# A cross network in two-level Winograd form: evicted blocks change buffers, and the second tile's transposes and loads change places

## The chip, the core and the metric

The kernel runs on one core of one Trainium2 chip. The metric is the device time of one execution in microseconds. The core has five engines that matter here: TensorE (PE) multiplies, ScalarE (ACT) and VectorE (DVE) work on tiles in SBUF and on the banks of PSUM in which PE leaves its results, GpSimd (POOL) and SyncE (SP) here mostly issue DMAs. Each engine runs its own program in order, and waits where a semaphore has not yet been raised.

## The reference: six cross layers

The input x0 has 16384 rows of 1024 features (bf16), there are six weight matrices of 1024 x 1024 and six biases. The output is x after the last layer.

```python
def reference(x0, ws, bs):
    x = x0
    L = ws.shape[0]
    for l in range(L):
        proj = jnp.einsum('bd,de->be', x, ws[l]) + bs[l]
        x = x0 * proj + x
    return x
```

## The kernel before

**Tiles and units.** Rows are cut into 16 tiles (`pr`) of 1024. Two tiles make a group, and the loop goes group by group, within a group layer by layer, and within a layer over the two tiles (`lane` 0 and 1). One tile in one layer is a unit: 96 units, numbered 0 to 95. Unit 12 g + 2 l + s is tile s of group g in layer l. So unit 37 is group 3, layer 0, second tile, and unit 38 is group 3, layer 1, first tile. The loop that writes all operations starts at line 268.

**Winograd.** In a unit x (1024 x 1024) and W (1024 x 1024) are each cut into four blocks of 512, and x W is done with seven block products instead of eight, P1 to P7. Each needs a weight block or a sum of such blocks, which the code names by the product ("1", "2", "4" raw; "5", "6", "7", "3" made by DVE). On the other side stand sums of x blocks, T1 to T4, made by DVE (lines 418 to 421). Three of the seven products (5, 2, 3), or four (also 4), are themselves done in seven quarter products, 5p1 to 5p7 and so on; their weight sums are "5i", "2i", "3i", "4i". Units of group 0's first tile and unit 95 are plain, that is without this second level; both tiles of layer 0 and the second tile of layers 1 to 4 have four inner products from group 1 on; the rest have three. A full product column is four matmuls of 512 columns at line 304 (`P1.0` is its first column group), an inner one four of 256 at line 492.

**Eviction.** PE writes eight PSUM banks, pA0 to pA3 and pX0 to pX3. ACT empties them: E1 into P1s, E6 into U, E7 into V, E4 into W (line 323, with the bias); the inner products by copies at line 313, of which some go from bank to bank (5f1, 5f2), some to `ip` (5e_p5), and some into a block (5e_c11, 5e_u0 and so on into 5c; the same for 2 into Q, 3 into 3c, 4 into W). The blocks are the seven tiles named `ev`: P1s, P5s (5c), Q, U, V, W, C3 (3c). Each role has its own fixed buffer (lines 171 and 172).

**After the products.** DVE adds the blocks up at line 199: 5cc, 2cc, 3cc, 4cc finish the inner products, then Q1 adds P1s to Q, Ua and Va add 5c to U and to V, Ub adds 3c to U, Wa adds V to W. Then Qm, Um, Vm, Wm multiply by x0. The old x is added last. In layers 1 to 4 that is an accumulating DMA of POOL for Q, U and V (`Qx`, `Ux`, `Vx`, lines 547 to 550), from the block into the state `xst`, and a DVE addition for W (`Wx`); in layer 5 DVE does all four; in layer 0 nothing, since the bias already has 1 added. So the buffer of U is read until Ux's DMA has landed, that of W until Wx is done.

**Weights.** Weight blocks pass through a ring of 12 slots (`wring`), in the order 1, 5, 5i, 2, 2i, 6, 3, 3i, 7, 4, 4i of each layer and group, and are used by both tiles. `pump` (line 234) issues a load on SP as soon as the oldest slot's last use has been emitted, so the load of a block waits, in SP's program, for a product of the second tile in the layer before: with 11 blocks to a layer and 12 slots, "5i" takes the slot of "5", "3i" that of "3". In group 0 only the raw blocks are loaded, DVE makes the sums and POOL saves them to DRAM (`Lc`).

**x0 and outputs.** x0 is kept in three tiles `x0T` and is loaded by transposing DMAs on SP, `ld` at line 328; those of the second tile are written in that tile's layer 0 unit (lines 341 to 343). A finished tile is transposed back by four DMAs `tro` (line 647) into a free x0T tile and stored by four `sto` (line 655). The first tile's output goes out in the second tile's layer 5 unit, that of the second tile (odd) in the next group's layer 0 unit of its second tile. After the odd tile's last `tro` POOL issues a tiny DMA, `fence` (line 338, tile `seen`), that waits for it; accumulating DMAs of POOL stand behind it.

**The order.** All operations are collected with the names of what they read and write (`op`, line 260). `schedule` (line 48) then simulates the five engines with the operations' `occ` (time on the engine) and `lat` (time to the result) and `at` (not before): PE follows the order written out at lines 17 to 36, every other engine takes the ready operation that is due first. The result is the order in which instructions are emitted, for all engines together (line 694). It sets each engine's program; on the chip the waits are by semaphores on the real buffers. `ARRIVE` holds the planner's assumed times of the first loads; an accumulating DMA is planned with a `lat` of 7.0 us.

Of the kernel before, what the change touches and what calls it, by code (L numbers as in the profile page):

```python
# [33 lines left out]
P1.0 P1.1 P1.2 P1.3 P2.0 P2.1 P2.2 P2.3 P5.0 P5.1 P5.2 P5.3 P6.0 P6.1 P6.2 P6.3 P3.0 P3.1 P3.2 P3.3 P7.0 P7.1 P7.2 P7.3  # L34
P4.0 P4.1 P4.2 P4.3 tV.0 tV.1 tV.2 tV.3 xW.0 tW.0 xW.1 tW.1 xW.2 tW.2 xW.3 tW.3
""".split()
ARRIVE = {"rows0": 4.9, "w0.1": 6.4, "rows1": 8.9, "rows2": 11.3, "w0.2": 11.9, "h0": 14.3, "h1": 15.5, "q": 17.5}


class Op:  # L40
# [85 lines left out]
def kernel(  # L126
# [12 lines left out]
    KH = KD // 2  # L139
    H = D // 2  # L140
# [28 lines left out]
    ip = {X: work.tile([P, KQ, KQ * P], BF16, name=f"ip{X}") for X in "523"}  # L169
    ip["4"] = ip["2"]  # L170
    P1s, P5s, Q, U, V, W, C3 = (work.tile([P, KH, KH, P], BF16, name=f"ev{i}") for i in range(7))
    CB = {"5": P5s, "2": Q, "3": C3, "4": W}
    TURNED, rows = ((0, 0), (1, 0), (0, 1)), (P1s, U, V)
    zeros = tin["4"][:, 0]
    ident = const.tile([P, P], BF16, name="ident")
# [45 lines left out]
    slot = {(gl, w): f"slot{i % RING}" for i, (gl, w, _) in enumerate(ring_seq)}  # L221
# [35 lines left out]
    ops, named = [], {}  # L257
    FAR = 1e9

    def op(name, eng, occ, lat, fn, rd=(), wr=(), weights=(), key=None, after=(), due=FAR, at=0.0):  # L260
        rd = tuple(rd) + tuple(slot[k] for k in weights if k in slot)
        for k in weights:
            uses_left[k] = uses_left.get(k, 0) + 1
        named[name] = len(ops)
        ops.append(Op(name, eng, occ, lat, fn, rd, tuple(wr), tuple(weights), key, tuple(named[a] for a in after), due, at))

    QD = ((0, 0), (0, 1), (1, 0), (1, 1))
    for u, (pr, l) in enumerate(units):
        one, first, last = plain(u), u == 0, u == NU - 1
        gl, grp, lane = gl_of(u), pr // 2, pr % 2  # L270
        x0T, xst = x0Ts[pr % 3], xsts[pr % 3]
        xs = x0T if l == 0 else xst
        X0 = {q: f"x0.{pr % 3}.{q[0]}{q[1]}" for q in QD}
        XO = {q: f"xs.{pr % 3}.{q[0]}{q[1]}" for q in QD}
# [14 lines left out]
        def dve(name, fn, n, rd, wr, weights=(), u=u, gl=gl, at=0.0, due=FAR):  # L289
            occ = n / 1920 + 0.068  # L290
            op(f"{name}@{u}", "DVE", occ, occ + 0.12, fn, rd, wr, [(gl, w) for w in weights], at=at, due=due)
# [33 lines left out]
        def load(pt, q, at=0.0, after=(), u=u):  # L325
            def fn():
                r0 = pt * PR + q[1] * NB
                nc.sync.dma_start_transpose(out=blk(x0Ts[pt % 3], *q), in_=x0[r0:r0 + NB, q[0] * H:(q[0] + 1) * H])
            op(f"ld{q[0]}{q[1]}.{pt}@{u}", "SP", 2.7, 6.0, fn, [], [f"x0.{pt % 3}.{q[0]}{q[1]}"], at=at, after=after)
# [10 lines left out]

        if l == 0 and lane == 1:
            for q in QD:
                load(pr, q, 17.0 if u == 1 else 0.0)

        if grp == 0 and lane == 0:
            raw = lambda w, gl=gl: wt[(gl, w)]

            def save(w, t, rd, weights=(), l=l, u=u, gl=gl):
                def fn():
                    nc.gpsimd.dma_start(Lc[l, CIDX[w]].rearrange("p (k e) -> p k e", k=KH), t())  # L350
                op(f"s{w}@{u}", "POOL", 1.0, 7.0, fn, rd + (["gate"] if u == 0 else []), (), [(gl, x) for x in weights])

            if first:
                ga = const.tile([P, 1], BF16, name="gate")

            def combo(w, a, b, o_, deps, gl=gl, raw=raw, first=first):
                def part(sl):
                    tt(raw(w)[:, :, sl], raw(a)[:, :, sl], raw(b)[:, :, sl], o_)

                def fn():  # L360
                    ring_make(gl, w)
                    part(slice(0, HQ) if w == "5" and first else slice(0, H))
                rd = [f"w{gl}.{d}" for d in deps]
                if w == "5" and first:
                    dve("c5", fn, KH * HQ, ["ringmake"], ["w0.5a", "ringmake", slot[gl, w]], [a, b], at=ARRIVE["h0"])
                    dve("c5b", lambda part=part: part(slice(HQ, H)), KH * HQ, ["w0.5a"], ["w0.5"], [a, b], at=ARRIVE["h1"])
                else:
                    dve("c" + w, fn, KH * H, rd + ["ringmake"], [f"w{gl}.{w}", "ringmake", slot[gl, w]], [a, b])
            combo("5", "w12", "4", ADD, ())
            combo("6", "5", "1", SUB, ("5",))  # L370
            combo("7", "1", "w12", SUB, ())
            combo("3", "2", "6", SUB, ("6",))
            for Xi in ISLOT:
                if Xi == "4i" and l not in K4:
                    continue
                X = Xi[0]
                a = lambda r, c, X=X, gl=gl: wt[(gl, X)][:, r * KQ:(r + 1) * KQ, c * HQ:(c + 1) * HQ]
                sv = isum(Xi).rearrange("p q (k e) -> p q k e", k=KQ)
                src = [] if X == "2" else [f"w{gl}.{5 if X == '4' else X}"]
                nm = lambda i, Xi=Xi: f"is.{Xi}.{i}"  # L380

                def icombo(i, fn, rd, Xi=Xi, X=X, src=src, nm=nm):
                    dve(Xi + i, fn, KQ * HQ, [nm(r) for r in rd] + src, [nm(i), ISN[Xi]], [X], at=ARRIVE["w0.2"] if first else 0.0)
                icombo("5", lambda a=a, sv=sv: tt(sv[:, 0], a(0, 1), a(1, 1), ADD), ())
                icombo("6", lambda a=a, sv=sv: tt(sv[:, 1], sv[:, 0], a(0, 0), SUB), "5")
                icombo("3", lambda a=a, sv=sv: tt(sv[:, 2], a(1, 0), sv[:, 1], SUB), "6")
                icombo("7", lambda a=a, sv=sv: tt(sv[:, 3], a(0, 0), a(0, 1), SUB), ())
# [8 lines left out]
        if first:  # L396
            for i, (d, n) in enumerate(TURNED):
                for k in range(KH):
# [8 lines left out]
                    f = lambda cp=cp, d=d, n=n, k=k, xb=xb, x0T=x0T: cp(out=blk(x0T, d, n)[:, k], in_=pX[xb][:])  # L407
# [15 lines left out]
        if not one:  # L423
            for X in inn:
                Bm, src = SRC[X]
                if kmajor:
                    q = lambda dh, n, Bm=Bm: Bm[:, dh * KQ:(dh + 1) * KQ, n * NQ:(n + 1) * NQ]
# [3 lines left out]
                else:  # L431
                    q = lambda dh, n, Bm=Bm: Bm[:, n * KQ:(n + 1) * KQ, dh * KQ:(dh + 1) * KQ, :].rearrange("p j k r -> p j (k r)")
# [29 lines left out]
        if not one:  # L462
            for X, a, b in (("5", 0, 1), ("2", 2, 3), ("3", 0, 1), ("4", 2, 3))[:len(inn)]:
                Bm, src = SRC[X]
                C, pn = CB[X], Pn[X]
                if kmajor:
                    q = lambda dh, n, k, Bm=Bm: Bm[:, dh * KQ + k, n * NQ:(n + 1) * NQ]
                    tk = lambda i, k, X=X: tin[X].rearrange("p i (k b) -> p i k b", k=KQ)[:, i, k]
                else:
                    q = lambda dh, n, k, Bm=Bm: Bm[:, n * KQ:(n + 1) * KQ, dh * KQ + k, :]  # L470
                    tk = lambda i, k, X=X: tin[X].rearrange("p i (j k r) -> p i j k r", j=KQ, k=KQ)[:, i, :, k, :]
                c = lambda dh, n, C=C: C[:, n * KQ:(n + 1) * KQ, dh * KQ:(dh + 1) * KQ, :].rearrange("p j m r -> p m j r")
# [60 lines left out]
        if not last:  # L533
# [8 lines left out]
            for nm, C, q in (("Q", Q, (0, 0)), ("U", U, (0, 1)), ("V", V, (1, 1)), ("W", W, (1, 0))):  # L542
                if l == 0:
                    ttop(nm + "m", xblk(xst, *q), C[:], x0j(*q), MULT, allm(nm) + [X0[q]], [XO[q]] + ISW)
                    continue
                ttop(nm + "m", C[:], C[:], x0j(*q), MULT, allm(nm) + [X0[q]], allm(nm))
                if nm in DMA_RES.get(l, ""):
                    def acc(C=C, q=q, xst=xst):
                        nc.gpsimd.dma_start(xblk(xst, *q), C[:], accum_op=ADD)  # L549
                    op(f"{nm}x@{u}", "POOL", 1.0, 7.0, acc, allm(nm) + [XO[q], "xbar"], [XO[q]])  # L550
                else:
                    ttop(nm + "x", xblk(xst, *q), C[:], xblk(xst, *q), ADD, allm(nm) + [XO[q]], [XO[q]])
        else:
# [86 lines left out]
        for pt, qs in outs:  # L640
            sp = (pt // 2 * 2 + 1) % 3 if pt < NPAIR - 2 else (pt - 1) % 3
            for q in qs:
                fl = x0Ts[sp][:, q[1], q[0] * KH:(q[0] + 1) * KH, :].rearrange("p k b -> p (k b)")
                sname = f"x0.{sp}.{q[0]}{q[1]}"

                def tro(q=q, pt=pt, fl=fl):
                    nc.sync.dma_start_transpose(out=fl.rearrange("p (f r) -> p f r", r=P),
                                                in_=xblk(xsts[pt % 3], *q).rearrange("p j k r -> p (j k r)"))
                op(f"tro{q[0]}{q[1]}.{pt}@{u}", "SP", 2.7, 6.0, tro, [f"xs.{pt % 3}.{q[0]}{q[1]}"], [sname])
                if pt % 2 and q == OUT[-1]:  # L650
                    fence(q, sp)

                def sto(q=q, pt=pt, fl=fl):
                    r0 = pt * PR + q[1] * NB
                    nc.sync.dma_start(out[r0:r0 + NB, q[0] * H:(q[0] + 1) * H].rearrange("(j p) f -> p j f", p=P),
                                      fl.rearrange("p (j f) -> p j f", j=KH))
                op(f"sto{q[0]}{q[1]}.{pt}@{u}", "SP", 0.5, 8.0, sto, [sname], ())
# [33 lines left out]
        load_half("4", h)  # L691
    nc.sync.dma_start_transpose(out=blk(x0Ts[0], 1, 1), in_=x0[NB:2 * NB, H:2 * H])

    for i in order:
        ops[i].fn()
        for k in ops[i].weights:
            if k in uses_left:
                uses_left[k] -= 1
        pump()
# [30 lines left out]
```

## Time and profile before

| What | Value |
| --- | --- |
| median of 3 runs | 2239.01 us (2235.86 to 2243.94) |
| the profiled execution | 2241.52 us, span 2239.8 us |
| mean granted TensorE clock | 0.998 |
| DMA | 478.66 MB in 454305 packets |
| weight loads of SP from `Lc` (line 242) | 329 of 512 KB, 6.9 us to landing (median) |
| output transposes of SP (line 647) | 60, 5.5 us to landing (median) |
| POOL accumulating DMAs (line 549) | 192 of 512 KB, 5.9 us to landing (median) |

A line of the profile names the engine, the line of the kernel, the operation and the tiles it writes and reads with buffer numbers left out, so that all seven blocks are called `ev` and all weight slots `wp`. In the answers by time, the first two columns are start and duration in us; a bracket at the end gives the engine's idle time before it and who ended it. Where waits are summed, the three numbers are the total in us, the number of waits, and the longest. Since DVE and ACT each run one line for many operations, single operations are told apart by their place in the engine's program.

### The profile page before, as it was taken

What the parts mean: (1) busy time and instruction counts of PE and PEld (TensorE: products, weight loads), DVE (VectorE), ACT (ScalarE), POOL (GpSimd) and SP (SyncE); (2) the same over time, 40 slices, a digit from 0 to 9 for tenths busy, and PEclk for the clock granted to TensorE, in tenths of its full rate; (3) what the DMA queues carried; (4) which work ended last, traced back from release to release, by engine and by line L of the source; (5) the groups of instructions that cost most, each with busy time, mean ns of one, the idle gap of its engine ahead of it and who ended that gap; (6) DMA issues with size and microseconds to landing.
All of it is one profiled execution on the core that took longest, in us unless ns stands there. A gap on an engine that the chain in (4) does not pass through costs nothing. (4 is left out here: it accounts for less than half of the span.)

```text
span 2239.8 us, 39440 instructions
## 1 busy us (share of the span) xinstructions
PE 2214.7 (99%) x14565; PEld 1421.0 (63%) x14565; DVE 2139.4 (96%) x2502; ACT 2027.2 (91%) x3627; POOL 205.9 (9%) x263
## 2 busy tenths in 40 slices
PE   8999999999999999999999999999999999999998
PEld 4555566666666666666666666666666666666664
DVE  7999999999999999999999999999999999999997
ACT  6888899999999999899999999999999999999997
POOL 2121100110001100011000110011100111001110
PEclk9999999999999999999999999999999999999999
DMA  8676897768976699766997669966799667996777
GB/s 247 220 206 193 207 219 241 199 170 213 250 251 179 173 233 244 237 179 176 238 261 227 170 183 243 278 190 174 202 246 278 173 179 217 240 258 170 198 221 164
DMA packets 454305, 478.66 MB, mean 214 GB/s; under 512 B 269024, under 2 KB 381152, under 8 KB 454112
## 3 DMA queue, kind: packets, MB, share of 16 engines
q1 hardware_dynamic: 418352, 349.49, 53.3%
q0 software_dynamic: 35168, 126.38, 26.7%
q8 instruction: 114, 1.87, 0.3%
q14 instruction: 79, 0.65, 0.1%
q10 hardware_dynamic: 592, 0.27, 0.0%
HBM read 252.72 MB, written 58.20 MB: 139 GB/s over the span
## 5 line engine op out<-in xcount | busy, mean ns | idle before, releaser
L492 PEld LDWEIGHTS <-wp 128*128 128x128 bf16 x8364 | 817.9, 98 | 284.7 <-DMA wp<-Lc 9.4
L323 ACT ACTIVATE ev<-pA,b_all 128x512 bf16<-128x512 f32 x1311 | 890.7, 692 | 118.3 <-PE pA L304 65.3
L304 PE MATMUL pA<-T,wp 128*128 128x512 bf16 x3936 | 940.5, 379 | 0.7 <-ACT ev L323 0.7
L304 PEld LDWEIGHTS <-wp 128*128 128x128 bf16 x5808 | 568.1, 98 | 509.9 <-issue 4.5
L313 ACT CAST ev<-pX 128x512 bf16<-128x512 f32 x1264 | 691.9, 595 | 39.0 <-PE pX L492 27.1
L492 PE MATMUL pX<-ti,wp 128*128 128x256 bf16 x4728 | 655.7, 273 | 7.1 <-DMA wp<-Lc 6.9
L199 DVE TENSOR_TENSOR ev<-ev,ev 128x2048 bf16<-128x2048 bf16 (+1 forms) x414 | 497.9, 1212 | 24.3 <-ACT ev L313 11.8
L199 DVE TENSOR_TENSOR ev<-ev,x0T 128x2048 bf16<-128x2048 bf16 (+1 forms) x324 | 383.9, 1202 | 0.7 <-ACT ev L323 0.3
L313 ACT COPY pX<-pX 128x512 f32<-128x512 f32 x618 | 357.7, 591 | 4.5 <-PE pX L492 0.3
L304 PE MATMUL pA<-xst,wp 128*128 128x512 bf16 x1280 | 318.9, 379 | 0.0
L549 POOL DMA_DIRECT2D xst<-ev x192 | 165.4, 862 | 1334.9 <-ACT pX L313 509.6
L492 PE MATMUL pX<-xst,wp 128*128 128x256 bf16 x1736 | 260.9, 273 | 2.5 <-ACT pX L313 2.5
L492 PE MATMUL pX<-T,wp 128*128 128x256 bf16 x1548 | 232.2, 273 | 0.0
L199 DVE TENSOR_TENSOR T<-xst,T 128x2048 bf16<-128x2048 bf16 x160 | 194.8, 1217 | 16.9 <-PE pX L492 16.1
L199 DVE TENSOR_TENSOR ev<-ev,ip 128x1024 bf16<-128x1024 bf16 x309 | 208.4, 682 | 1.4 <-ACT ev L313 1.4
L199 DVE TENSOR_TENSOR T<-xst 128x2048 bf16<-128x2048 bf16 x160 | 194.6, 1216 | 7.6 <-DMA xst<-ev 5.3
L313 ACT CAST ip<-pX 128x512 bf16<-128x512 f32 x309 | 182.3, 590 | 7.9 <-PE pX L492 7.9
L199 DVE TENSOR_TENSOR xst<-ev,xst 128x2048 bf16<-128x2048 bf16 x124 | 150.5, 1218 | 1.2
L199 DVE TENSOR_TENSOR ti<-xst 128x1024 bf16<-128x1024 bf16 x148 | 101.0, 684 | 14.8 <-PE pX L492 14.8
L199 DVE TENSOR_TENSOR ti<-T,ti 128x512 bf16<-128x512 bf16 x262 | 108.8, 415 | 0.2
L199 DVE TENSOR_TENSOR ti<-xst,ti 128x1024 bf16<-128x1024 bf16 x148 | 101.2, 684 | 1.0
L199 DVE TENSOR_TENSOR ti<-T 128x1024 bf16<-128x1024 bf16 x131 | 89.2, 681 | 0.1
(57 smaller groups left out, 677.9 us busy)
## 6 DMA issues: line engine op xcount, KB each, us to landing
wp<-Lc SPq DMA_DIRECT2D x329, 512.0 KB, 6.9
xst<-ev POOLq DMA_DIRECT2D x192, 512.0 KB, 5.9
wp<-in_ws_dram SPq DMA_DIRECT2D x148, 512.0 KB, 7.2
out_dram<-x0T SPq DMA_DIRECT2D x60, 512.0 KB, 5.5
Lc<-wp POOLq DMA_DIRECT2D x24, 512.0 KB, 5.9
Lc<-xst POOLq DMA_DIRECT2D x23, 512.0 KB, 3.5
ev<-in_x_dram SPq DMA_DIRECT2D x3, 512.0 KB, 6.2
wp<-in_ws_dram SPq DMA_DIRECT2D x4, 256.0 KB, 7.3
```

The lines of the kernel that those rows point to most:

```text
L199: nc.vector.tensor_tensor(out=o, in0=a, in1=b, op=op)
L304: nc.tensor.matmul(o, lhsT=wt[(gl, w)][:, k, m * P:(m + 1) * P], rhs=r, start=(start and k == 0), stop=(k == KH - 1), skip_group_check=True)
L313: act(name, lambda: nc.scalar.copy(out=dst, in_=src), rd, wr)
L323: act(name, lambda: nc.scalar.activation(out=dst, in_=src, func=IDENT, bias=b_all[:, c:c + 1], scale=1.0), rd, wr, True)
L492: nc.tensor.matmul(o if kmajor else o.rearrange("p (j r) -> p j r", r=P), lhsT=wv[:, k, m * P:(m + 1) * P], rhs=rhs(k), start=(start and m ...
L549: nc.gpsimd.dma_start(xblk(xst, *q), C[:], accum_op=ADD)
```

## The change

Buffers. The roles 5c, 3c, U, V, W, Q and P1s no longer have fixed buffers. From each unit to the next U takes the buffer that W had, V that of U, W that of V, and 5c and 3c change places; Q and P1s stay. The names that the planner sees follow (`at_home`).

The planner's numbers. An accumulating DMA is planned with 9.0 instead of 7.0 us, the second tile's first x0 loads not before 21.0 (was 17.0), the sums on layer 1's raw weights not before 40.0 (was 0).

Order. The odd tile's four output transposes come, in the planner, after the first column group of P7 of the unit in which they stand. The second tile's four x0 loads of group 0 are emitted ahead of all planned operations, and so ahead of layer 1's raw weights.

```diff
-..., "q": 17.5}
+..., "q": 17.5, "next": 21.0, "raw1": 40.0}
+ACCUM = 9.0
...
-    CB = {"5": P5s, "2": Q, "3": C3, "4": W}
+    EV = {"5c": P5s, "3c": C3, "U": U, "V": V, "W": W, "Q": Q, "P1s": P1s}
+    NEXT = {"5c": "3c", "3c": "5c", "U": "W", "V": "U", "W": "V", "Q": "Q", "P1s": "P1s"}
+    home = {r: r for r in EV}
...
+    def at_home(r):
+        p, dot, m = r.partition(".")
+        return home[p] + dot + m if p in home else r
+
     def op(name, eng, occ, lat, fn, rd=(), wr=(), weights=(), key=None, after=(), due=FAR, at=0.0):
+        rd, wr = [at_home(r) for r in rd], [at_home(r) for r in wr]
...
+        if not first:
+            home = {r: home[NEXT[r]] for r in home}
+        P1s, P5s, Q, U, V, W, C3 = (EV[home[r]] for r in ("P1s", "5c", "Q", "U", "V", "W", "3c"))
+        CB = {"5": P5s, "2": Q, "3": C3, "4": W}
...
-                load(pr, q, 17.0 if u == 1 else 0.0)
+                load(pr, q, ARRIVE["next"] if u == 1 else 0.0)
...
-                    dve("c" + w, fn, KH * H, rd + ["ringmake"], [f"w{gl}.{w}", "ringmake", slot[gl, w]], [a, b])
+                    dve("c" + w, fn, KH * H, rd + ["ringmake"], [f"w{gl}.{w}", "ringmake", slot[gl, w]], [a, b], at=ARRIVE["raw1"] if gl == 1 else 0.0)
...
-                    op(f"{nm}x@{u}", "POOL", 1.0, 7.0, acc, allm(nm) + [XO[q], "xbar"], [XO[q]])
+                    op(f"{nm}x@{u}", "POOL", 1.0, ACCUM, acc, allm(nm) + [XO[q], "xbar"], [XO[q]])
...
-                op(f"tro{q[0]}{q[1]}.{pt}@{u}", "SP", 2.7, 6.0, tro, [f"xs.{pt % 3}.{q[0]}{q[1]}"], [sname])
+                op(f"tro{q[0]}{q[1]}.{pt}@{u}", "SP", 2.7, 6.0, tro, [f"xs.{pt % 3}.{q[0]}{q[1]}"], [sname],
+                   after=[f"P7.0@{u}"] if pt % 2 else [])
...
+    held = [i for i in order if ops[i].name.startswith("ld") and ops[i].name.endswith(".1@1")]
+    for i in held:
+        ops[i].fn()
     for i in order:
-        ops[i].fn()
+        if i not in held:
+            ops[i].fn()
```

More of the change, by code (lines that the diff above doesn't have):

```diff
@@ L36 @@
 """.split()
-ARRIVE = {"rows0": 4.9, "w0.1": 6.4, "rows1": 8.9, "rows2": 11.3, "w0.2": 11.9, "h0": 14.3, "h1": 15.5, "q": 17.5}
+ARRIVE = {"rows0": 4.9, "w0.1": 6.4, "rows1": 8.9, "rows2": 11.3, "w0.2": 11.9, "h0": 14.3, "h1": 15.5, "q": 17.5, "next": 21.0, "raw1": 40.0}
+ACCUM = 9.0
 class Op:
```

## The prediction

> **What bounds the kernel now.** I read the busy shares first, then who TensorE waits for, then TensorE in order of time, then the engine named at each gap.
>
> ```profile
> PE 2214.7 (99%) x14565; PEld 1421.0 (63%) x14565; DVE 2139.4 (96%) x2502; ACT 2027.2 (91%) x3627; POOL 205.9 (9%) x263
> ```
>
> TensorE (PE) is the bound: only its gaps can be won. How large they are is read from unit starts. The first matmul of unit 1 starts at 35.44, that of unit 95 at 2204.73. Undisturbed units last 24.17 (plain), 22.98 (three inner products) and 22.59 us (four); units 1 to 94 hold 5, 47 and 42 of these, 2149.7 in all, against 2169.3 used. So 19.6 us is all that the change can win between unit 1 and the tail. The waits divide it:
>
> ```profile
> PE pX L492 <- DMA wp<-Lc: 6.9, 6, 2.0
> PE pX L492 <- ACT pX L313: 5.0, 6, 2.5
> PE pX L304 <- ACT pX L313: 1.1, 3, 0.5
> PE pA L304 <- ACT ev L323: 0.7, 2, 0.5
> ```
>
> Idle time understates a stop: a matmul after one takes 0.38 where the stream's pitch is 0.216, so 0.17 is added to each; I count from start to start. TensorE's rows in time show the three kinds:
>
> ```profile
> 44.20 0.60 PE L492 MATMUL pX<-T,xst 128*128 128x256 bf16 x4 [2.52 <-ACT pX L313]
> 521.62 0.60 PE L492 MATMUL pX<-xst,wp 128*128 128x256 bf16 x4 [0.70 <-ACT pX L313]
> 905.42 1.27 PE L492 MATMUL pX<-ti,wp 128*128 128x256 bf16 x8 [2.02 <-DMA wp<-Lc]
> ```
>
> Kind 1, 44.20, in unit 1: 2.7 us. ScalarE (ACT) and VectorE (DVE) say why:
>
> ```profile
> 42.59 0.58 ACT L313 CAST ev<-pX 128x512 bf16<-128x512 f32 x1 [2.79 <-DVE ev L199]
> 32.26 1.23 DVE L199 TENSOR_TENSOR wp<-wp 128x2048 bf16<-128x2048 bf16 x1 [2.30 <-DMA wp<-in_ws_dram]
> 36.51 0.69 DVE L199 TENSOR_TENSOR ti<-x0T 128x1024 bf16<-128x1024 bf16 x1 [1.88 <-DMA x0T<-in_x_dram]
> 41.26 1.21 DVE L199 TENSOR_TENSOR ev<-ev,ev 128x2048 bf16<-128x2048 bf16 x1
> ```
>
> The eviction 5e_c11 of unit 1 writes the 5c buffer that Va of unit 0 (41.26) still reads; Va is late by DVE's two waits, 2.30 for layer 1's raw weights and 1.88 for the second tile's x0.
>
> Kind 2, 521.62 and its like: ACT waits for an accumulating DMA to let go of a buffer.
>
> ```profile
> 519.92 0.69 ACT L323 ACTIVATE ev<-pA,b_all 128x512 bf16<-128x512 f32 x1 [1.19 <-DMA xst<-ev]
> 1370.85 1.26 ACT L323 ACTIVATE ev<-pA,b_all 128x512 bf16<-128x512 f32 x2 [1.52 <-DMA xst<-ev]
> ```
>
> The first is E7.0 of an odd unit waiting for the V DMA (Vx) of the unit before, the second E6.0 of an even unit waiting for Ux. Start to start these cost 3.8 us (eight stops in odd units) and 1.5 (units 58, 64, 92): 5.3. Unit 4 loses 0.5 to a wait for Qx's DMA.
>
> Kind 3, 905.42: weights late in the first tile's layer 1 unit of a group. SyncE's (SP's) queue ahead of it:
>
> ```profile
> 875.95 5.33 SPq L647 DMA_TRANSPOSE x0T<-xst  x1
> 881.33 0.58 SPq L242 DMA_DIRECT2D wp<-Lc  x1
> 881.95 7.42 SPq L647 DMA_TRANSPOSE x0T<-xst  x2
> 889.41 0.59 SPq L242 DMA_DIRECT2D wp<-Lc  x1
> ...
> 895.13 3.03 SPq L242 DMA_DIRECT2D wp<-Lc  x2
> ```
>
> One weight load gets out between 875.95 and 889.41, though slots come free from unit 37's P1.3 (876.1) on; the other loads then queue on each other, and "3i" (issued 895.13) lands 10.2 us later, at 905.37. The kind costs 10.3: 1.9 in unit 26, 4.9 in units 37 and 38, 1.6 in 50, 1.2 in 74, 0.7 in 14, 62 and 86. Of the 4.9, 1.7 is a slow clock: the granted clock over 893 to 920 is 0.94 (0.06 x 27), and it comes nowhere else but at the end, so I count it to these stops.
>
> [...]
>
> 2.7 + 5.3 + 10.3 = 18.3; the other 1.3 are unit 4's 0.5 and scattered stops of 0.1 to 0.2.
>
> **The change, part by part.**
>
> x0 ahead of layer 1's weights. Nothing is added: four transposing loads and four 512 KB weight loads change places on SP. Now three x0 loads go out from 14.37 to 21.8, four weight loads until 24.1, then the fourth x0 load. After it, x0 is out by about 24.3 (2.5 each by 7.45/3) and the weights by 26.5. The fourth x0 lands some 6 earlier than its 36.5; the weights about 2.5 later, at 34.7 by 32.26 + 2.4, and the first sum on them is now planned at 40. They are needed in unit 2, at 58, so that costs nothing; if the cover went, DVE would wait again, as at 32.26. Both DVE waits go: 4.2 us, off the path except through Va.
>
> Rotation. No instruction is added. What each first writer of unit u+1 waits for becomes: 5c waits for Ub of u (was Va); 3c for Va (was Ub); U for Wx or Wm on DVE (was Ux's DMA); V for Ux's DMA (was Vx's); W for Vx's DMA (was Wx). I put times from the start of u+1, naming ACT's and DVE's rows by the kernel's order.
> - 5c in unit 1 gets C3, which unit 0 does not use: the 2.79 wait goes, and with it 2.7 on PE. The Va that is late next has until unit 1's 3e_c11, at 15.7.
> - E7.0 of odd units stands at 16.27; Ux has landed at 7.3 to 9.5, so its wait goes. Late next is 4e_c11 at 16.85, behind Vx, which lands at 14.8 to 17.3 (five of 28 after 16.9, by up to 0.5). Queued behind it on ACT are 3f2 and 4f2, due 0.3 later: 3.8 falls to 0.4.
> - E6.0 of even units waited until 13.9 to 15.5; Wx ends at 10.9, and P7.0, which needs the bank, starts at 15.76: 1.5 falls to 0. Q's buffer does not move, so unit 4's 0.5 stays.
> - E6.0 of odd units, now at 9.76, waits for Wx at 9.5 to 10.5, or 12.3 to 13.9 around layers 5 and 0. P7.0 starts at 15.2 there, so E6.0 may start as late as 14.4. Price 0 by the order that stands; a late Wx would hold 3e_p5 and 5e_c21 behind E6.0, and E6's four rows of 0.6 come closer together.
> - 5c after a four-product unit: Va ends at 3.96, Ub at 5.09, 5e_c11 starts at 4.25, and 5p3 needs it by 4.78 (5p3 at 6.07 less two copies). Ub needs 3cc, ready at 1.05, and now stands behind Wa and Va, which can wait. The planner knows the buffer names, so Ub moves ahead. Bounds: 0, and 47 us (a rival below). I take 0, by the nearest row: Va met the same deadline with 0.3 to spare.
> DVE's results reach PE at least 3.7 us early in every unit from 12 on, so its order can move.
>
> The planner's figure for an accumulating DMA goes from 7 to 9 us; measured issue to landing is 5.9 median and 7.5 to 9.7 for Vx of even units. It shifts order alone: bounded by -0.4 (the residue above) and +2 (the scattered stops of 0.8 more than doubled). I take +2 for all reordering, as I can't see the new order.
>
> Output transposes after P7.0. The four transposes of the odd tile (3.6 us each on SP, 60 rows of 1.3 to 7.3) now go out 24.1, 17.4, 11.4 and 6.8 us before unit 38 starts; they move behind unit 37's P7.0 (8.1 before) in program order, and no semaphore is added. They pass the loads of "5i", "2", "2i", "6" and "3", whose slots unit 37's 5p4 to P6.2 free (880 to 884): these go out with nothing ahead. Three transposes occupy SP from 8.0 before unit 38 (its start is 0 here) to +2.8, by 3.6 each. The fourth, and the stores, come behind "3i", since its slot opens with 3p4, unit 37's last product: in the planner the fourth follows P7.0 by 3 x 2.7 = 8.1, and 3p4 starts 5.9 after P7.0's result (22.15 against 15.2 + 0.86 + 0.19). So "3i" goes out at +2.8 and lands 4.4 later (median of 20 first loads behind a transpose, 3.6 to 7.1): +7.2, needed at +9.7. With 12.7 for the three (the slowest here, 5.33 + 4.50 + 2.82) and 5.7, it is 0.7 late. 10.3 falls to 0.5. POOL's fence waits for the fourth transpose, landing near +12; behind it is Qx of unit 38 at +16.7 and all later accumulating DMAs: 4 us of cover.
>
> [...]
>
> **Sum**, against the profiled execution's 2241.5 (span 2239.8, 1.7 around it): 2.7 + (5.3 - 0.4) + (10.3 - 0.5) = 17.4, less 2 for reordering is 15.4, and so 2226.1; I say 2226. That is 13 (0.58%) under the median 2239.0, which lies 2.5 under the profiled run already.
>
> **Rivals.** 0.3% (6.7 us, limit 2232.3) is about what can be told from no change.
> - Weights stay late. For it: the 16 DMA engines are full then (share 1.12 and 1.08 in units 36 and 37), and moving transposes removes no bytes; single transposes hold SP for up to 7.3. Against: one transpose and four stores leave the stretch ahead of "3i". The 9.8 stays: 2235.8, same.
> - Rotation gives nothing beyond unit 1, 4e_c11 inheriting E7.0's wait and E6.0 finding Wx as late as Ux: 4.9 stays, 2230.9, faster.
> - Slower: Ub stays behind Va. Then 5e_c11 starts at 5.16 instead of 4.78 after each of 28 four-product units in layers 1 to 4: 0.38 x 28 = 10.6; after layer 0's units Ub ends at 8.9 and 6.7 against 5.65 and 4.78 for the start: 3.3 x 7 + 1.9 x 7 = 36.4. Together 47: 2273. It decides once the mean lateness passes 0.31 over these 42 borders (13 in all). Against it: the order is made anew with the new names.
> - The transposes wait only in order, not by semaphore; if SP reached them early, nothing would change in kind 3: 2235.8 again, counted with the first.
>
> **Numbers.** As forecast 0.57 (2222 to 2230; 2222 is all 19.6 won), weights late 0.17, rotation void beyond unit 1 0.10, slower 0.11, another new wait of 7 to 10 us with no change to show 0.05. Faster 0.57 + 0.09 + 0.02 = 0.68; same 0.20; slower 0.12. The first three make 0.84 and span 2222 to 2235.8; with half a us below and one above for spread among runs it is 2221.5 to 2237.
>
> **What would show it.** Right: unit 1 near 23.0 and no wait for DVE ev at 42; no row of ACT ev L323 <- DMA xst over 0.6; layer 1's first units at 23.0 and no half clock at 906; SP's transposes in two groups of four, the second some 8 us before that unit. Wrong: 5e_c11 rows waiting for DVE ev; "3p5" waiting for DMA wp still; POOL's seen later than unit start + 16.

## The result, and the profile after

The changed kernel takes 2222.18 us (median of 4 runs, 2222.11 to 2222.44) against 2238.65 for the kernel before (4 runs, 2235.86 to 2243.94). The ratio is 0.9924, with a 95% interval of 0.9905 to 0.9942: 16.5 us faster. The spread from run to run, 8.1 us before, is 0.3 now. The profiled execution took 2222.17, its span is 2220.2.

The busy shares and all waits of TensorE in the changed kernel (line numbers have moved by 5 to 14: 199 is now 204, 304 is 318, 313 is 327, 323 is 337, 492 is 506, 647 is 661; after a wait come its total in us, the number of waits and the longest):

```profile
PE 2209.2 (100%) x14565; PEld 1421.3 (64%) x14565; DVE 2133.0 (96%) x2502; ACT 2035.8 (92%) x3627; POOL 204.6 (9%) x263
```

```profile
PE pX L681 <- DVE ti L678: 1.2, 1, 1.2
PE pX L318 <- ACT pX L327: 0.8, 2, 0.5
PE pX L318 <- DVE T L204: 0.6, 1, 0.6
PE pX L417 <- DVE x0T L421: 0.6, 1, 0.6
PE pA L318 <- ACT x0T L421: 0.4, 1, 0.4
PE pX L417 <- DMA ev<-in_x_dram: 0.2, 1, 0.2
```

The reader is to see what is missing: no wait for weights (`wp<-Lc`, 6.9 before), none of an inner product for a bank (5.0 before), none for E6 (0.7 before). All six lie in the first 19 us: the first is the very start, where TensorE waits for VectorE's first instruction, the others are in unit 0. Unit 1 starts at 35.38 and unit 95 at 2186.05; the units between take 2150.7 against the 2149.7 of undisturbed ones. So of the 19.6 us that the prediction had found to win there, 18.6 are gone. The span is shorter by 19.6 too, which is chance: 18.6 here, 0.9 in the tail (34.15 from unit 95's start to the end, 35.07 before), 0.1 ahead of unit 1.

SyncE's queue ahead of unit 38, which now starts at 886.47:

```profile
878.41 0.32 SPq L247 DMA_DIRECT2D wp<-Lc  x1
878.77 9.40 SPq L661 DMA_TRANSPOSE x0T<-xst  x3
888.27 1.20 SPq L247 DMA_DIRECT2D wp<-Lc  x2
889.57 0.38 SPq L247 DMA_DIRECT2D wp<-in_ws_dram  x1
890.04 0.46 SPq L247 DMA_DIRECT2D wp<-Lc  x1
890.59 0.41 SPq L247 DMA_DIRECT2D wp<-in_ws_dram  x1
891.06 7.00 SPq L661 DMA_TRANSPOSE x0T<-xst  x1
```

All earlier weight loads are out by 878.7. Three transposes fill SP from 7.7 before the unit to 1.7 after it, then "3i" goes out at once (888.27) and lands 5.66 after the unit's start, 3.9 before its product. The fourth transpose comes behind it. The granted clock is 1.00 from the start to 2216.4 us, behind the last matmul.

### The profile page after: what moved, and what is told of

Same layout as the page of the kernel before. It is cut to its first block, busy times and chain, and to the rows that moved or that the text cites. A ratio compares the mean times of both kernels' runs of the same rounds, so it can differ in the third digit from the quotient of the medians.

```text
span 2220.2 us, 39424 instructions
## 1 busy us (share of the span) xinstructions
PE 2209.2 (100%) x14565; PEld 1421.3 (64%) x14565; DVE 2133.0 (96%) x2502; ACT 2035.8 (92%) x3627; POOL 204.6 (9%) x263
## 4 chain that ended last, share of the span: by engine, by line
PE 98%; DMA 1%; SPq 0%; DVE 0%; issue 0%; POOLq 0%; ACT 0%; DVEq 0%; ACTq 0%
PE pA L318 53%; PE pX L506 43%; PE pX L318 3%; DMA x0T<-in_x_dram 0%; DMA xst<-x0T 0%; SPq L690 0%; DVE ev L204 0%; SPq L697 0%; DVE x0T L204 0%; DVE T L204 0%; SPq L703 0%; POOLq L744 0%; ACT ev L337 0%; SPq L700 0%; DVEq L204 0%
```

## The experiments

Every ratio is against runs of the kernel before on the same chip, with its 95% interval. Since the changed kernel has almost no stops, losses are given against its 2222.2 (medians). A "stop" is measured on TensorE from start to start.

### Leaving one part out

**no_rot**: all buffers stay fixed, the rest of the change is there.

```diff
-    NEXT = {"5c": "3c", "3c": "5c", "U": "W", "V": "U", "W": "V", "Q": "Q", "P1s": "P1s"}
+    NEXT = {"5c": "5c", "3c": "3c", "U": "U", "V": "V", "W": "W", "Q": "Q", "P1s": "P1s"}
```

> The changed kernel with fixed buffers again; all else stays. My theory: the waits of ACT for accumulating DMAs come back (E7.0 of odd units behind Vx, E6.0 of even units behind Ux), 5.3 us in the run before, so about 2227.5; unit 1 stays near 23.0, because x0 now comes early and Va of unit 0 is in time without the spare buffer. Rival: the planner's 9.0 for an accumulating DMA alone makes the order that avoids them: 2222 to 2223, and no row of ACT waiting for DMA xst over 0.6 us.

Measured: 2267.52 us, ratio 1.0125 [1.011, 1.014]. That is 45.3 slower than with the rotation, and slower than the kernel before; no theory had this. Unit 1 is clean here, with fixed buffers, so the early x0 alone removes kind 1 too. Waits of TensorE, then ScalarE in time around one stop, then TensorE there (unit 28 starts at 665.03):

```profile
PE pA L318 <- ACT ev L337: 38.4, 28, 1.4
PE pX L506 <- ACT pX L327: 2.4, 6, 0.4
```

```profile
678.50 0.57 ACT L327 COPY pX<-pX 128x512 f32<-128x512 f32 x1
680.49 1.07 ACT L327 CAST ev<-pX 128x512 bf16<-128x512 f32 x2 [1.42 <-PE pX L506]
681.45 4.23 ACT L337 ACTIVATE ev<-pA,b_all 128x512 bf16<-128x512 f32 x7
```

```profile
682.20 2.75 PE L318 MATMUL pA<-T,wp 128*128 128x512 bf16 x12 [1.37 <-ACT ev L337]
```

ScalarE waits 1.42 us for TensorE (the copies 3e_u0 and 3e_u1) while TensorE is about to wait for ScalarE (E6.0 at 681.45, which P7.0 needs for its bank). Nothing of a DMA ends here: the Ux transfer that E6.0 must wait for had landed at 679.48, 2 us before. The stop is in the order. With fixed buffers and 9.0 us for an accumulating DMA, the kernel's own schedule expects U free only 16.37 us after the unit's start, when 3e_u0 and 3e_u1 (planned at 15.38 and 16.02) have been begun, and so puts E6.0 behind them in ScalarE's program. The chip then keeps to that order although U is free early. There are 28 such stops of 1.53. Six more of 0.56 come before 5p3 in layer 1's first tiles, and the schedule plans these too (5p3 of unit 26 at 6.59 after the unit's start instead of 6.07). Together 46.2.

**no_tro**: the odd tile's output transposes don't wait for P7.0.

```diff
-                op(f"tro...", "SP", 2.7, 6.0, tro, [...], [sname],
-                   after=[f"P7.0@{u}"] if pt % 2 else [])
+                op(f"tro...", "SP", 2.7, 6.0, tro, [...], [sname])
```

> The changed kernel with the odd tile's output transposes planned as soon as they are ready, as before. My theory: 3p5 in the first tile's layer 1 units waits for weights again, 10.3 us with the half clock in the profiled run of before, so about 2232 with several us of spread between runs; units 38, 50 and 74 over 24 us. Rival: the late weights came from the earlier stops and from the old order of accumulating DMAs, and stay away: 2222 to 2224.

Measured: 2244.46 us, ratio 1.0025 [1.0015, 1.0034]; 22.3 lost, twice what I had counted for late weights. The waits of TensorE and SyncE's queue ahead of unit 38 (it starts at 890.72):

```profile
PE pX L506 <- DMA wp<-Lc: 15.3, 10, 2.8
```

```profile
883.88 1.57 SPq L247 DMA_DIRECT2D wp<-Lc  x1
885.50 0.50 SPq L247 DMA_DIRECT2D wp<-in_ws_dram  x1
886.11 5.29 SPq L661 DMA_TRANSPOSE x0T<-xst  x1
891.44 1.05 SPq L247 DMA_DIRECT2D wp<-Lc  x2
```

In the kernel before the last transpose left SP 4.0 us ahead of the unit, here 0.7 after its start. The rotation and the 9.0 have reordered layer 5, and a block that these transposes read is finished later: DVE adds the old x to U of unit 35 until 16.7 us into unit 36, where it was 9.4 before. So the size of this part depends on the others: in rot_only it is larger still, in accum_only (below) there is no late weight at all.

**no_x0**: the second tile's x0 behind layer 1's weights again, with the planner's old numbers.

```diff
-..., "next": 21.0, "raw1": 40.0}
+..., "next": 17.0, "raw1": 0.0}
...
-    held = [i for i in order if ops[i].name.startswith("ld") and ops[i].name.endswith(".1@1")]
+    held = []
```

> The changed kernel with the second tile's x0 loads and layer 1's raw weights planned and emitted as before. My theory: rotation alone clears unit 1, since 5c goes to a buffer nobody reads: unit 1 at 23.0, DVE's two waits of about 2 us back but harmless, 2222.5. Rival: DVE's 4 us make another eviction or a T of units 1 to 3 late: 2224 to 2226.

Measured: 2227.36 us, ratio 0.9945 [0.993, 0.996]; 5.2 lost, more than either theory had. VectorE's two waits are back, ahead of unit 1, and what they lead to stands in unit 4, in ScalarE's and in TensorE's rows:

```profile
32.24 1.23 DVE L204 TENSOR_TENSOR wp<-wp 128x2048 bf16<-128x2048 bf16 x1 [2.15 <-DMA wp<-in_ws_dram]
36.71 0.69 DVE L204 TENSOR_TENSOR ti<-x0T 128x1024 bf16<-128x1024 bf16 x1 [3.24 <-DMA x0T<-in_x_dram]
...
115.66 0.69 ACT L337 ACTIVATE ev<-pX,b_all 128x512 bf16<-128x512 f32 x1 [6.58 <-DMA xst<-ev]
...
116.88 1.86 PE L318 MATMUL pX<-xst,wp 128*128 128x512 bf16 x4 [4.96 <-ACT pX L327]
```

Unit 1 itself is clean, so the exchange of 5c and 3c alone removes kind 1. But VectorE is busy without a break from 40 to 80 us (20.00 of 20 in both halves, as in the changed kernel), so it doesn't catch up there: Q of unit 3 is ready late, its accumulating DMA goes out at 106.15 instead of 101.19, and unit 4's E2.0 waits for it.

**no_accum**: an accumulating DMA is planned with 7.0 us, as before.

```diff
-ACCUM = 9.0
+ACCUM = 7.0
```

> The changed kernel with 7.0 instead of 9.0 us planned for an accumulating DMA. My theory: only order moves; Vx of even units again goes out behind Ux and lands at 15 to 17 us, 4e_c11 waits at times: 2222.2 to 2223. Rival: 9.0 is what puts V first and holds the stops away: 2224 to 2227, with ACT waiting for DMA xst at 4e_c11.

Measured: 2234.34 us, ratio 0.9981 [0.9972, 0.999]; 12.2 lost, again more than either theory had. Waits of VectorE, then one chain in time through VectorE, ScalarE and TensorE:

```profile
DVE T L204 <- DMA xst<-ev: 22.5, 19, 3.3
DVE ti L204 <- DMA xst<-ev: 2.9, 3, 1.6
```

```profile
654.31 1.23 DVE L204 TENSOR_TENSOR T<-xst 128x2048 bf16<-128x2048 bf16 x1 [1.01 <-DMA xst<-ev]
...
663.26 3.49 DVE L204 TENSOR_TENSOR ev<-ev,ev 128x2048 bf16<-128x2048 bf16 x3
...
665.73 0.58 ACT L327 CAST ev<-pX 128x512 bf16<-128x512 f32 x1 [0.90 <-DVE ev L204]
...
667.35 0.60 PE L506 MATMUL pX<-T,wp 128*128 128x256 bf16 x4 [0.63 <-ACT pX L327]
```

A sum for the next unit stands in VectorE's program where the plan has its input landed; on the chip it is not, and VectorE stands still for 1.01 with other work queued behind. From there VectorE runs 1.05 behind its plan. Eleven us later a block (Ub's, which 5e_c11 is to overwrite) is released late, ScalarE waits 0.90, TensorE 0.63. Nine stops before 5p3 make 6.7 of the loss. The changed kernel has two such waits of VectorE, of 0.2 and 0.3. Its 192 accumulating DMAs land 4.5 to 9.7 us after issue, nine in ten within 7.7.

### One part alone

**rot_only**: the kernel before with the rotation (7.0, no early x0, no wait for P7.0).

```diff
+    NEXT = {"5c": "3c", "3c": "5c", "U": "W", "V": "U", "W": "V", "Q": "Q", "P1s": "P1s"}
...
+        if not first:
+            home = {r: home[NEXT[r]] for r in home}
+        P1s, P5s, Q, U, V, W, C3 = (EV[home[r]] for r in ("P1s", "5c", "Q", "U", "V", "W", "3c"))
```

> The kernel before with the rotation alone: 7.0 for accumulating DMAs, transposes and x0 loads as before. My prediction's step priced the rotation at 2.7 + 4.9 us: 2231. The theory that the last four runs leave (rotation only makes room; without the 9.0 the planner puts Ub and Vx late, and the transposes then block the weights for longer): 2242 to 2255, slower than before, with ACT waiting for DVE ev at 5e_c11.

Measured: 2278.82 us, ratio 1.017 [1.0149, 1.0191]: 39 us slower than the kernel before, and beyond the 2242 to 2255 expected. The step that I had priced as a gain of 7.6 is a loss when it stands alone. Waits of TensorE:

```profile
PE pX L506 <- DMA wp<-Lc: 25.3, 8, 5.8
PE pX L506 <- DVE ev L204: 6.5, 2, 3.5
PE pX L318 <- ACT pX L327: 6.0, 3, 5.3
```

Most of it is weights: with the new names the order of layer 5 changes, the last early transposes leave SP 3.8 us before unit 38, and "5i" lands as that unit begins. The second line is more of the same: these are the starts of units 38 and 86, 0.05 after "5i" landed. The third line is unit 4 as in no_x0. The mean granted clock is 0.991, against 0.999 in the changed kernel.

**x0_tro**: early x0 and the wait for P7.0, with fixed buffers and 7.0.

```diff
-    NEXT = {"5c": "3c", "3c": "5c", "U": "W", "V": "U", "W": "V", "Q": "Q", "P1s": "P1s"}
+    NEXT = {"5c": "5c", "3c": "3c", "U": "U", "V": "V", "W": "W", "Q": "Q", "P1s": "P1s"}
...
-ACCUM = 9.0
+ACCUM = 7.0
```

> The changed kernel with fixed buffers and 7.0, so only the x0 loads and the odd tile's transposes are moved. Theory (these two don't need the rotation): unit 1 at 23.0, no wait for weights; ACT's waits for accumulating DMAs (5.3) and the scattered stops (1.3) stay: 2228. Rival (all parts work only together, as the losses of 5 to 45 us suggest): 2236 and over.

Measured: 2232.6 us (2227.71 to 2236.45 over 10 runs), ratio 0.9962 [0.995, 0.9974]. Unit 1 is clean and no weight is late. What is left is nearly all kind 2. ScalarE's waits here, and then in no_accum, which differs from x0_tro by the rotation alone:

```profile
ACT ev L337 <- DMA xst<-ev: 13.9, 22, 2.2
```

```profile
ACT ev L337 <- DMA xst<-ev: 2.2, 6, 0.6
```

So the rotation does take the waits for accumulating DMAs off ScalarE when 7.0 is planned, as forecast. It wins nothing by it (2234.34 against 2232.6), because VectorE's waits for the same DMAs grow from 5.2 us in 12 places to 22.5 in 19. The profiled execution of x0_tro (2228.18) loses 6.0, the median run 10.4 against the changed kernel. Its runs spread by 8.7 us, as much as those of the kernel before; that kind 2 is what varies is likely, but only one execution was profiled.

**accum_only**: the kernel before with 9.0 and nothing else.

```diff
-                    op(f"{nm}x@{u}", "POOL", 1.0, 7.0, acc, ...)
+                    op(f"{nm}x@{u}", "POOL", 1.0, 9.0, acc, ...)
```

> The kernel before with 9.0 instead of 7.0 us planned for an accumulating DMA and nothing else. Theory: with fixed buffers a landing after 9.0 does not fit, so the planner itself plans a stop of 1.6 us before P7.0 of 28 units, and ACT keeps that order on the chip however early the DMA lands: 1.53 in each of these units as without rotation, 2275 to 2285. Rival: the chip's landings (5.9 median) decide, not the plan: 2237 to 2241.

Measured: 2271.01 us, ratio 1.0138 [1.0119, 1.0157]. Waits of TensorE:

```profile
PE pA L318 <- ACT ev L337: 38.3, 28, 1.4
PE pX L506 <- ACT pX L327: 5.0, 7, 2.6
```

The same 28 stops as in no_rot, the six of 0.56, and unit 1 with 2.8: 49.0. One number in the planner, with no instruction added or taken, costs 31 us. No weight is late here: in this order the early transposes leave SP 10.4 before unit 38.

**copy_early**: the changed kernel without the wait for P7.0, and the odd tile's four transposing DMAs made plain copies of the same bytes at that early place (so that the odd tiles' output is not turned back).

```diff
+                    (nc.sync.dma_start_transpose(...) if pt % 2 == 0 else
+                     nc.sync.dma_start(fl, xblk(xsts[pt % 3], *q).rearrange("p j k r -> p (j k r)")))
-                op(f"tro...", ..., [sname], after=[f"P7.0@{u}"] if pt % 2 else [])
+                op(f"tro...", ..., [sname])
```

> The changed kernel without the transposes' wait for P7.0, in which the odd tile's four transposing DMAs are plain copies of the same bytes at the same place in the program (so the odd tiles' output is not turned back). Theory SP's program: a copy holds SP for 0.5 us instead of 3.6, the weight loads behind it go out in time, 2222 to 2224. Rival DMA engines: the bytes are what makes the weights late, units 38, 50 and 74 stay over 24 us, 2235 to 2244.

Measured: 2222.22 us, ratio 0.992 [0.9899, 0.9942], against 2244.46 for no_tro, which differs only in the transposing. SyncE's queue, same place:

```profile
871.99 1.31 SPq L663 DMA_DIRECT2D x0T<-xst  x1
873.35 1.32 SPq L247 DMA_DIRECT2D wp<-Lc  x1
874.71 1.21 SPq L670 DMA_DIRECT2D out_dram<-x0T  x1
875.97 0.69 SPq L247 DMA_DIRECT2D wp<-Lc  x1
876.70 0.50 SPq L247 DMA_DIRECT2D wp<-in_ws_dram  x1
877.31 0.92 SPq L663 DMA_DIRECT2D x0T<-xst  x1
```

The two copies in these rows hold SP for 1.31 and 0.92 us, the last two transposes of no_tro ahead of the same unit held it for 3.73 and 5.29. The bytes and their place in the order are the same, and the DMA engines are as full: over the 12 us from 8 before unit 38 their share is 1.04 here and 1.05 in no_tro (389 and 272 GB/s). "2i" goes out 8.4 before the unit here and 0.7 after its start in no_tro, and once out it lands after 9.8 us here and 4.5 there. So the weights were late because they went out late, behind transposes in SP's program, and not because full engines moved them slowly. What holds SP for so long in a transposing DMA no run shows.

### Which half, and how much

**acc8**: 8.0 instead of 9.0.

```diff
-ACCUM = 9.0
+ACCUM = 8.0
```

> The changed kernel with 8.0 us planned for an accumulating DMA. Theory (the plan must cover the chip's landing, or DVE and ACT stand still in order behind a DMA): with 7.0 DVE waited 25 us in 22 places and the loss was 12; landings of 7 to 8.5 are mostly covered by 8.0: 2222.2 to 2225. Rival (only 9.0 happens to give a good order): 2228 and over.

Measured: 2222.73 us, ratio 0.9923 [0.9908, 0.9938]. With 8.0 one stop of 0.69 is left, so the loss lies between 7.0 and 8.0.

**uvw_only** and **swap_only** take the rotation apart: U, V and W rotate while 5c and 3c stay, and the other way round.

```diff
-    NEXT = {"5c": "3c", "3c": "5c", "U": "W", "V": "U", "W": "V", "Q": "Q", "P1s": "P1s"}
+    NEXT = {"5c": "5c", "3c": "3c", "U": "W", "V": "U", "W": "V", "Q": "Q", "P1s": "P1s"}   # uvw_only
+    NEXT = {"5c": "3c", "3c": "5c", "U": "U", "V": "V", "W": "W", "Q": "Q", "P1s": "P1s"}   # swap_only
```

> The changed kernel with U, V and W rotating and 5c and 3c fixed. Theory (a plan whose landings are covered is run as planned): the planner's own stops on PE are 5.4 us instead of 1.3, mostly 0.52 before 5p3 of layer 1's first tiles, so 2226.3. Rival (the swap matters little, or much more than planned): 2222 or over 2230.

> The changed kernel with 5c and 3c changing places and U, V and W fixed. Theory: the planned stops are 12.4 instead of 1.3 us (0.36 before P7.0 in 28 units, the rest elsewhere), so 2233. Rival: as without any rotation, 2260 and over, or 2222.

Measured: uvw_only 2229.11 us, ratio 0.9952 [0.9936, 0.9969]; swap_only 2222.42, ratio 0.9921 [0.9906, 0.9936]. Either half removes the 28 stops before P7.0. U, V and W alone leave 6.9: stops before 5p3, six of 0.56 in layer 1's first tiles and six of 0.3 to 0.6 in layer 0's second ones, and 1.2 in the tail. The exchange of 5c and 3c alone leaves nothing, so with 9.0 planned U, V and W need not move. This refuted what I had taken from no_rot, that any planned wait at P7.0 comes true. ScalarE around unit 28 in swap_only (the unit starts at 658.73):

```profile
672.21 0.57 ACT L327 COPY pX<-pX 128x512 f32<-128x512 f32 x1
672.69 1.85 ACT L337 ACTIVATE ev<-pA,b_all 128x512 bf16<-128x512 f32 x3
674.41 0.60 ACT L327 CAST ev<-pX 128x512 bf16<-128x512 f32 x1
```

E6.0 (672.69) runs straight after 3f2, 13.96 into the unit, ahead of 3e_u0 (674.41); in no_rot it ran at 16.42, behind it. The kernel's schedule still plans a stop of 0.36 before P7.0 in 28 units, but the order is good, and Ux lands at 11.3 after the unit's start (670.03), so none occurs. What brings Ux forward is the new name of 5c: Ub now reads the buffer that the next unit's 5e_c11 writes, so it is due early, goes ahead of Va, and Ux leaves at 6.76 instead of 7.66.

**held_only**: x0 emitted first, but the planner's two start times as before.

```diff
-..., "next": 21.0, "raw1": 40.0}
+..., "next": 17.0, "raw1": 0.0}
```

> The changed kernel with the x0 loads emitted first, but planned at 17.0, and with the sums on layer 1's raw weights planned from 0 on, as before. Theory (a DVE wait in units 0 and 1 is carried by a full DVE to unit 4): DVE waits 4 to 5 us for the raw weights, Qx of unit 3 goes out late and E2.0 of unit 4 waits for it: 2225 to 2228. Rival: x0's landing was what counted, 2222 to 2223.

Measured: 2225.59 us, ratio 0.9936 [0.9921, 0.9951]; 3.4 of the 5.2 of no_x0 stay lost. Waits of VectorE:

```profile
DVE wp L204 <- DMA wp<-in_ws_dram: 3.6, 1, 3.6
```

Moving the loads is not enough: the sums on layer 1's raw weights must also go back in VectorE's order, or VectorE waits for the loads that were put behind.

## Why the prediction came out as it did

Time, direction and range were right (2226.1 worked out, 2222.2 measured). The 3.9 between them: reordering was priced at +2 and left 0.98 (six stops of 0.16 at 4p4); the residues of 0.4 and 0.5 were 0; the 1.3 of unit 4 and scattered stops went too, with 0.9 in the tail and 0.1 ahead of unit 1; 0.3 more lies around the span. The sum held better than its terms. That the order made with all parts at once has hardly a stop was luck as far as the prediction goes: it could not see the new order, and orders made with single parts are 31 to 39 us slower than before.

- **Unit 1** (2.7): right, and twice over: it is clean without the x0 part (no_x0) and without the rotation (x0_tro). But DVE's two waits were not "off the path except through Va": with VectorE full to 80 us they reach unit 4, worth 5.2 in the changed kernel. The 2.5 later weights cost nothing only because the sums on them were moved (held_only).
- **Rotation, kind 2** (5.3 less 0.4): the mechanism was right, but it is not the only one, and the account stopped at ScalarE. At 7.0 the rotation cuts ScalarE's waits from 13.9 to 2.2 us (x0_tro, no_accum), yet VectorE then stands at landings and the gain is lost. At 9.0 only one such wait, of 0.8 us, is left even with fixed buffers (no_rot), but there the schedule has stops of its own, and the kernel takes 34.9 us longer than at 7.0 (x0_tro). Only both together leave nothing, and then the exchange of 5c and 3c is all that is needed of the rotation (swap_only); whether it is enough at 7.0 was not tried. The size came from one execution; the median run of x0_tro loses 10.4.
- **Ub ahead of Va**: right, in the plan and on the chip. Ub ends 4.17 and 5e_c11 starts 4.28 after the start of most even units. The slower rival did not occur here; at 7.0 it does in part, with eight waits of 5e_c11 for VectorE of 0.5 to 0.9 in no_accum, though Ub stands ahead of Va there too.
- **The 7 to 9 us**: the step that failed. "It shifts order alone, bounded by -0.4 and +2" was right in its first half and far off in the second: 12.2 gained beside the rotation (no_accum), 31 lost when it stands alone (accum_only), 34.9 lost beside the other two parts with fixed buffers (x0_tro to no_rot). An assumed time of DMAs in the planner moves evictions and additions past one another on every engine, and the prediction priced that by the stops of the old order.
- **Transposes** (10.3 less 0.5): right in the mechanism and nearly in its times: three transposes from -7.7 to +1.7 (forecast -8.0 to +2.8), "3i" landed at 5.66 (7.2). The rival of full DMA engines is out: they are as full in copy_early (share 1.04 against 1.05 in no_tro), where nothing is late. 22 us hang on SP's time (2244.46 against 2222.22): 3.73 and 5.29 for a transpose there, 0.92 and 1.31 for a copy. The 10.3 itself belongs to one order.
- **POOL's fence**: wrong in detail. It does not wait for the fourth transpose; the quarter that it needs is planned first, and it runs 1.1 before unit 38. That costs nothing either way.
- **The half clock** (1.7 of the 10.3) went with the stops, as counted: the kernel before was granted 0.50 from 906.1 to 909.5, the changed kernel 1.00 up to 2216.4.

The parts do not add. The four losses of leaving one out come to 45.3 + 22.3 + 5.2 + 12.2 = 85, five times the 16.5 that the whole change gains, and two parts done alone lose 39 and 31. My sum was right for the kernel in which all the stops are gone at once, since that floor (19.6) was read from unit starts, and not because each term was right. Why the tail is 0.9 shorter stays open: it is 34.0 to 34.2 us in the changed kernel, accum_only and no_tro, 35.0 to 35.2 in the kernels with 7.0, but 35.1 and 35.3 also in swap_only and uvw_only with 9.0.

## What to carry to other kernels

Where a program fixes the order of in-order engines from assumed latencies, price a latency by what it moves ahead of what: too short, and engines stand at inputs that have not landed (12 us here, beside the rotation); too long without a free buffer, and work is put behind other work and stays there though its input is early (31 to 35 us). Look at the idle engine just before a stop: if it waits for the engine that is about to wait for it, as in no_rot, look for the fault in the order before you look at a transfer. And bound a change of several parts by the floor of its undisturbed units before adding up the parts.

## What the runs showed of the hardware beyond this

The half clock came after a stop shorter than its own stretch. In the kernel before TensorE is idle for 2.02 us ahead of 905.42; the granted clock is 1.00 up to 906.1, 0.50 from there to 909.5, so for 3.4 us, and 1.00 again behind it. TensorE of no_tro, in time:

```profile
619.37 1.75 PE L506 MATMUL pX<-ti,wp 128*128 128x256 bf16 x8 [2.13 <-DMA wp<-Lc]
```

These eight matmuls take 1.75 us, where eight such take 1.04 in the changed kernel (886.03, no stop ahead). The mean granted clock of this execution is 0.997, that of the changed kernel 0.999. Twenty-eight stops of 1.5 in accum_only leave its mean at 0.999; a stretch of 3.4 us at half behind each would have made it 0.98. Nor did the stop in unit 1 of the kernel before bring one, with 2.52 us of idle time ahead of 44.20: the granted clock is 1.00 from 40 to 61. So the length of a stop alone does not decide; what does, no run shows.

An accumulating DMA of 512 KB landed anywhere from 4.5 to 9.7 us after its issue in the changed kernel. Once the order allowed for that, the spread of the whole kernel fell from 8.1 to 0.3 us, so the scatter between runs of the kernel before probably came from waits that end with a landing. The other kernels agree: those with such waits spread by 2.0 to 8.7 (held_only, accum_only in unit 1, no_x0, no_accum, rot_only, no_tro, x0_tro), while no_rot, which loses 45 us to stops that its order fixes, spreads by 0.3.
